# The first expert's first half on the first 384 tokens: one pass of 384 columns, or three of 128

## The chip, the cores and the metric

The kernel runs on one core of a Trainium2 chip. The metric is the device time of one execution in microseconds (us). Five engines work beside each other, each with a queue of its own that it takes in order: TensorE (PE, whose weight loads have a row of their own, PEld), VectorE (DVE), ScalarE (ACT), GpSimd (POOL) and SyncE (SP), which here issues all DMAs.

## The reference

Attention with a decay, a mixture of eight experts whose weights for each token are balanced over all tokens, and a gated layer behind it:

```python
scores = scale * q @ k.T + (cum[:, None] - cum[None, :]); causal mask
attn = softmax(scores);  x = attn @ v            # 2 batches, 8 heads, 576 tokens, head size 64
P = balance(exp(x @ w_gate))                     # 1152 tokens x 8 experts, 8 rounds over rows and columns
for e in range(8):
    out += P[:, e:e+1] * (relu(x @ w1[e]) @ w2[e])   # 512 -> 1024 -> 512
h = out @ w_in;  g = h * tanh(softplus(h));  return g @ w_out
```

All numbers are 32-bit. To keep precision at TensorE's faster number type, an operand is split into a high and a low part, and a product is three matmuls: high x high, low x high, high x low.

## The kernel before

Attention goes by query tiles: ten, five for each batch. Eight hold 128 rows, and one of each batch holds 64. Each tile has four units of two heads, so there are 40 units, and the loop in line 702 goes in half units: steps `s` = 0 to 87, `pi, a = divmod(s, 2)`. Tile `ti` has the steps 8 ti to 8 ti + 7. In the text the tiles are counted from one: the first has the steps 0 to 7. The program is written out in this order, and each engine takes its part of it in order. A step issues the exponential of the step before (ACT), the score matmuls (PE, then a masked reduction on DVE), dummy matmuls, one filler piece (`fill`, line 650), and, in odd steps, the attention product of three units back (`attend`) and the transposes of two units back. Then come the splits, transposes and copies of the next tile's queries and keys (`prep`), and DMA loads.

Dummy matmuls multiply the identity with itself. `warm` (line 391) issues one or two in each of the first 16 steps, and `warm_late` (line 396) one in steps 17, 19, 21, 25 and 27.

The filler is work of the expert stage that is put between attention's matmuls. Its weights are those of the first half of the first expert (512 of 1024 hidden units), loaded in four parts of 512 KB (`Weights.load`, line 52) into two staging buffers (tag `stg`, one of which first holds the raw second query and key tile, `early`), and split in eight pieces by `split_w` (line 322): the high part on ACT or DVE, whichever `pick` thinks is freer, and the low part on DVE. Tokens go in chunks of 384, three query tiles each in the first chunk. `filler(c)` (line 604) can start when the last tile of chunk c is attended. For each of four blocks of 128 hidden units it issues 12 matmuls of 384 columns, three to a piece, then evicts them: ReLU on ACT, low part on DVE. Then, for each of three token tiles, four pieces of three 512-wide matmuls, and an eviction into `acc`. That is 28 pieces, one a step: steps 31 to 58 for chunk 0, from step 63 on for chunk 1. Chunk 2 follows behind attention (line 825).

The weights for the filler are loaded when unit 7 starts (step 14) and split one piece at a time in every second step from 24 on; the third and fourth part are loaded as the buffers come free (`wsplit`, line 680).

Of the kernel before, what the change touches and what calls it, by code (L numbers as in the profile page):

```python
# [8 lines left out]
F32 = mybir.dt.float32  # L9
FR = mybir.dt.float32r  # L10
AF = mybir.ActivationFunctionType
ALU = mybir.AluOpType
# [26 lines left out]
def f(ap):  # L39
    return ap.bitcast(F32)  # L40
# [43 lines left out]
def attention_moe_kernel(  # L84
# [44 lines left out]
    with ExitStack() as actx:  # L129
# [165 lines left out]
        def spent(engine, ns):  # L295
            busy[engine] += ns
# [6 lines left out]
        def evac(o, i, cols, scale=None):  # L303
            if pick(act=90 + 0.83 * cols, dve=90 + 1.05 * cols) == "act":
                if scale:
                    nc.scalar.activation(out=o, in_=i, func=AF.Copy, scale=scale)
                else:
                    nc.scalar.copy(out=o, in_=i)
            elif scale:
                nc.vector.tensor_scalar(out=o, in0=i, scalar1=scale, scalar2=None, op0=ALU.mult)  # L310
            else:
                nc.vector.tensor_copy(out=o, in_=i)
# [80 lines left out]
            for _ in range(n):  # L393
                nc.tensor.matmul(out=wt[:, :128], lhsT=idn, rhs=idn, start=True, stop=True)  # L394

        def warm_late(n):

            late = ps_f.tile([128, 512], F32, tag="fb", name="late")
            for _ in range(n):
                nc.tensor.matmul(out=late[:, :128], lhsT=idn, rhs=idn, start=True, stop=True)  # L400

        def scores_two(u, a):
            b, h, nk = u["b"], u["h"], u["nk"]
            slot, k0 = u["slots"][h // 4], kbase[b]
# [153 lines left out]
        def attend(u):  # L558
            n, nk, h, b, pT = u["n"], u["nk"], u["h"], u["b"], u["pT"]
            if h == 0:  # L560
                u["tile"]["x"] = ps_x.tile([128, 4, 128], F32, tag="x", name="x")
            x = u["tile"]["x"]
            nblk = (nk + 127) // 128
            for j in range(nblk):
                w = 128 if j == 4 else min(128, nk - 128 * j)
                for a in range(2):
                    nc.tensor.matmul(  # L567
                        out=x[64 * a:64 * a + 64, h // 2, :n], lhsT=vts[b, j][:w, h + a, :],
                        rhs=pT[:w, 128 * j + 64 * a:128 * j + 64 * a + 64] if n == 64 else pT[:w, a, j * n:(j + 1) * n],
                        start=j == 0, stop=j == nblk - 1,  # L570
                    )
            if h == H - 2:
                c, t0 = divmod(b * S + u["s0"], CH)
                nc.scalar.copy(out=xh[c][:, :, t0:t0 + n], in_=x[:, :, :n])
                nc.vector.tensor_tensor(
                    out=xl[c][:, :, t0:t0 + n], in0=x[:, :, :n], in1=f(xh[c][:, :, t0:t0 + n]), op=ALU.subtract
                )
                spent("act", 90 + 3.4 * n)
                spent("dve", 90 + 4.2 * n)
# [16 lines left out]
        def gate_end(c, lg):  # L596
# [4 lines left out]
            nc.vector.tensor_copy(out=gl, in_=lt[:, :, E:])  # L601
            nc.vector.tensor_tensor(out=P[:, 3 * c:3 * c + 3], in0=lt[:, :, :E], in1=gl, op=ALU.add)

        def filler(c):

            w = wts.slots[0]
            if c == 0:
                hs = [
                    tuple(t[2][:, i].rearrange("p (j t) -> p j t", j=3) for t in (xh, xl)) for i in range(4)
                ]  # L610
            else:
                hs = []
                for i in range(4):
                    h0, c0 = 3 * (i % 2), 576 + 128 * (i // 2)
                    hs.append(tuple(t[:, h0:h0 + 3, c0:c0 + 128] for t in (kt, kbf)))
            for i in range(4):
                fs = slice(i * 128, (i + 1) * 128)
                ph = ps_f.tile([128, 512], F32, tag="fb", name="ph")[:, :CH]
                for kk in range(KD):
                    for n, (wn, x) in enumerate((("w1h", xh), ("w1h", xl), ("w1l", xh))):  # L620
                        nc.tensor.matmul(  # L621
                            out=ph, lhsT=w[wn][kk][:, fs], rhs=x[c][:, kk],
                            start=(kk == 0 and n == 0), stop=(kk == KD - 1 and n == 2),
                        )
                    if kk == KD - 1:
                        hh, hl = hs[i]
                        p3 = ph.rearrange("p (j t) -> p j t", j=3)
                        nc.scalar.activation(out=hh, in_=p3, func=AF.Relu)
                        nc.vector.scalar_tensor_tensor(
                            out=hl, in0=p3, scalar=0.0, in1=f(hh), op0=ALU.max, op1=ALU.subtract  # L630
                        )
                        spent("act", 400)
                        spent("dve", 500)
                    yield
            for j in range(3):
                pa = ps_f.tile([128, 512], F32, tag="fb", name="pa")
                for i in range(4):
                    hh, hl = hs[i]
                    for n, (a_, wn) in enumerate(((hh, "w2h"), (hh, "w2l"), (hl, "w2h"))):
                        nc.tensor.matmul(  # L640
                            out=pa, lhsT=a_[:, j], rhs=w[wn][i],
                            start=(i == 0 and n == 0), stop=(i == 3 and n == 2),
                        )
                    if i == 3:
                        evac(acc[c * 3 + j], pa, 512)
                    yield
# [32 lines left out]

        def wsplit(i):  # L680
            wts.split(0, i // 2, i % 2, how=split_w)
            if i % 2 and i < 5:
                wts.load(0, i // 2 + 2, stage)

        (qs0, qt0), (ks0, kt0) = make_preps(0)
        qs0(0)
# [15 lines left out]
        for s in range(2 * nu + 8):  # L702
# [11 lines left out]
                scores(units[pi], a)  # L714
            if s < 16:
                warm((2,2,2,2,2,2,2,2,1,1,1,1,1,1,1,1)[s])
            elif s in (17,19,21,25,27):
                warm_late(1)
            fill()
            fills += ready  # L720
            ready = []
            if a and 3 <= pi < nu + 3:
                w = units[pi - 3]
                attend(w)
                if w["h"] == H - 2 and w["ti"] in (2, 6, 9):
                    c = (2, 6, 9).index(w["ti"])
                    gates.append(c)
                    if c < 2:
                        ready.append(filler(c))
                elif gates:  # L730
                    logits.append(gate(gates.pop(0)))
            elif logits:
                gate_end(*logits.pop(0))
# [31 lines left out]
                    kt_(1)  # L765
            if late_rows and s >= 2:
                late_rows.pop(0)()
            if a:
                continue
            s = pi  # L770
            if s == 3:
                nc.gpsimd.tensor_copy(out=wgc[:, :, 0, :], in_=wg)
                nc.gpsimd.tensor_tensor(out=wgc[:, :, 1, :], in0=wg, in1=f(wgc[:, :, 0, :]), op=ALU.subtract)
            if s == 7:
                wts.load(0, 0, stage)
                wts.load(0, 1, stage)
            if s == 8:
                cum_k(1, 0, 256)
            if s == 22:
                cum_k(1, 256, 576)  # L780
            if s >= 12 and wtasks:
                wtasks.pop(0)()
        while gates:
            logits.append(gate(gates.pop(0)))
        fill(2)
# [1098 lines left out]
```

## Time and profile before

| | us |
|---|---|
| median of three runs | 1094.47 |
| the three runs | 1094.47, 1094.21, 1099.45 |
| profiled execution, span | 1097.7 |
| PE busy | 1090.1 |
| DVE busy | 839.7 |
| ACT busy | 541.6 |
| POOL busy | 75.3 |

The rows are of one profiled execution; its time is given by the span from its first to its last instruction, and no row gives what lies around it. The attention stage ends near 168 us of the span; the expert stage and the gated layer fill the rest. The ends of matmuls are modelled, so PE looks busy also where it waits a little; the starts of matmuls, one behind the other, tell more.

### The profile page before, as it was taken

How to read it: one execution, taken by the hardware profiler on the slowest of the kernel's cores; microseconds unless marked ns; L12 is line 12 of the kernel's file. 1: busy time of each engine (PE TensorE's matmuls, PEld its weight loads, DVE VectorE, ACT ScalarE, POOL GpSimd, SP SyncE). 2: the span in 40 equal slices, each digit the busy share in tenths (PEclk: the TensorE clock that was granted, in tenths of full speed). 3: DMA queues.
4: the chain of work that ended last, by engine and by line, in shares of the span. 5: the costliest groups of instructions: out<-in, count | busy, mean ns of one | idle time of the engine just before them, and what ended most of it. 6: DMA issues, size and time to landing. Idle time of an engine off the chain costs nothing.

```text
span 1097.7 us, 18374 instructions
## 1 busy us (share of the span) xinstructions
PE 1090.1 (99%) x6838; PEld 970.0 (88%) x6838; DVE 839.7 (76%) x1891; ACT 541.6 (49%) x1287; POOL 75.3 (7%) x124
## 2 busy tenths in 40 slices
PE   9999999999999999999999999999999999999998
PEld 8788778988989899898989989898898989899997
DVE  7755646878797887977888796888877559778994
ACT  7756642354435252443524335252443448877881
POOL 6534420000000000000000000000000000000000
PEclk9799999999999999999999999999999999999999
DMA  6534302022342424325243343424323341261502
GB/s 147 134 78 108 87 11 87 1 89 78 123 135 77 144 83 149 121 87 158 91 151 98 127 137 109 153 85 147 102 100 96 106 162 42 76 202 51 171 1 87
DMA packets 103805, 114.98 MB, mean 105 GB/s; under 512 B 35236, under 2 KB 63860, under 8 KB 103716
## 3 DMA queue, kind: packets, MB, share of 16 engines
q1 hardware_dynamic: 103716, 113.81, 33.6%
q8 instruction: 54, 0.88, 0.3%
q14 instruction: 35, 0.29, 0.1%
HBM read 82.24 MB, written 27.07 MB: 100 GB/s over the span
## 4 chain that ended last, share of the span: by engine, by line
PE 98%; DVE 1%; ACT 1%; issue 0%; POOL 0%; DVEq 0%; POOLq 0%
PE bank L855 33%; PE bank L1265 29%; PE bank L1737 9%; PE bank L1647 4%; PE ph L825 3%; PE x L567 3%; PE bank L1576 2%; PE spare L1647 2%; PE pa L855 2%; PE pa L640 2%; PE ph L621 1%; PE sp L467 1%; PE pt L360 1%; PE pt L531 1%; PE wt L394 1%; PE sp L468 1%
## 5 line engine op out<-in xcount | busy, mean ns | idle before, releaser
L855 PE MATMUL bank<-w2h,big 128*128 128x512 f32 x924 | 300.2, 394 | 0.0
L855 PEld LDWEIGHTS bank<-w2h,big 128*128 128x128 f32 x924 | 173.8, 188 | 38.7 <-DVE hid_b L833 0.2
L855 PE MATMUL bank<-w2l,big 128*128 128x512 f32 x528 | 207.5, 393 | 0.0
L1294 ACT COPY snap<-bank 128x288 f32<-128x288 f32 x168 | 66.6, 396 | 175.2 <-PE bank L1265 174.8
L855 PEld LDWEIGHTS bank<-w2l,big 128*128 128x128 f32 x528 | 99.3, 188 | 20.9
L832 ACT ACTIVATE big<-c 128x288 fp32r<-128x288 f32 x168 | 74.9, 446 | 83.7 <-DVE c L1299 79.7
L833 DVE SCALAR_TENSOR_TENSOR big<-c,big 128x288 fp32r<-128x288 f32 x140 | 64.0, 457 | 57.1 <-ACT big L832 54.5
L1030 DVE SCALAR_TENSOR_TENSOR acc<-bank,P,acc 128x512 f32<-128x512 f32 x132 | 92.3, 744 | 18.8 <-PE bank L855 18.8
L1265 PE MATMUL bank<-tt,ss 128*128 128x288 f32 x672 | 103.2, 295 | 0.0
L1265 PE MATMUL bank<-xh,ss 128*128 128x288 f32 x448 | 103.1, 295 | 0.0
L1265 PEld LDWEIGHTS bank<-tt,ss 128*128 128x128 f32 x672 | 93.9, 188 | 0.0
L1299 DVE TENSOR_TENSOR c<-bank,snap 128x288 f32<-128x288 f32 x168 | 75.8, 451 | 20.1 <-PE bank L1265 19.7
L1011 ACT CAST hb<-da 128x512 fp32r<-128x512 f32 x38 | 23.7, 624 | 107.4 <-DVE da L986 96.0
L1265 PEld LDWEIGHTS bank<-xh,ss 128*128 128x128 f32 x448 | 76.6, 188 | 0.0
L1265 PE MATMUL bank<-xl,ss 128*128 128x288 f32 x224 | 66.5, 297 | 0.0
L1265 PE MATMUL bank<-xh,w1l 128*128 128x288 f32 x224 | 66.2, 296 | 0.0
L1265 PE MATMUL bank<-xl,w1h 128*128 128x288 f32 x224 | 66.2, 295 | 0.0
L1265 PE MATMUL bank<-xh,w1h 128*128 128x288 f32 x224 | 66.1, 295 | 0.0
L75 DVE TENSOR_TENSOR w2l<-stg,w2h 128x512 fp32r<-128x512 f32 x60 | 41.2, 689 | 14.6 <-ACT w2h L74 14.1
L855 PE MATMUL bank<-w2h,hid_b 128*128 128x512 f32 x132 | 51.7, 391 | 0.0
L511 POOL TENSOR_SCALAR p<-p,rs 128x256 f32<-128x256 f32 (+5 forms) x72 | 42.0, 595 | 68.7 <-DVE rs L507 47.5
L1265 PE MATMUL bank<-tt,w1h 128*128 128x288 f32 x224 | 46.3, 295 | 0.0
(314 smaller groups left out, 2467.4 us busy)
## 6 DMA issues: line engine op xcount, KB each, us to landing
stg<-in_moe_w_dram SPq DMA_DIRECT2D x64, 512.0 KB
wb<-w_in_b SPq DMA_DIRECT2D x42, 256.0 KB
raw<-in_moe_w_in_dram SPq DMA_DIRECT2D x16, 512.0 KB
raw<-in_moe_w_out_dram SPq DMA_DIRECT2D x16, 512.0 KB
w_in_b<-hb SPq DMA_DIRECT2D x18, 256.0 KB
w_out_h<-hb SPq DMA_DIRECT2D x16, 256.0 KB
w_out_l<-da SPq DMA_DIRECT2D x16, 256.0 KB
w_in_f<-da SPq DMA_DIRECT2D x12, 256.0 KB
```

What stands on the lines that cost most here:

```text
L75: (lo_engine or nc.vector).tensor_tensor(out=lo, in0=raw, in1=f(hi), op=ALU.subtract)
L511: nc.gpsimd.tensor_scalar(out=p[:n, a, :nk], in0=p[:n, a, :nk], scalar1=r[:n, a:a + 1], scalar2=1.0, op0=ALU.mult, op1=ALU.mult,)
L567: nc.tensor.matmul(out=x[64 * a:64 * a + 64, h // 2, :n], lhsT=vts[b, j][:w, h + a, :], rhs=pT[:w, 128 * j + 64 * a:128 * j + 64 * a + 64] ...
L832: nc.scalar.activation(out=hh, in_=ph, func=AF.Relu)
L833: nc.vector.scalar_tensor_tensor(out=hl, in0=ph, scalar=0.0, in1=f(hh), op0=ALU.max, op1=ALU.subtract)
L855: nc.tensor.matmul(out=pa, lhsT=a_[:, ts_], rhs=w[wn][ft_], start=(first and n == 0), stop=(last and n == 2),)
L1030: nc.vector.scalar_tensor_tensor(out=acc[t], in0=pa, scalar=P[:, t, e:e + 1], in1=acc[t], op0=ALU.mult, op1=ALU.add)
L1265: nc.tensor.matmul(out=by_chunk(out_) if len(v_.shape) == 3 else out_, lhsT=u, rhs=v_, start=first and m == 0, stop=m == 5, skip_group_che ...
L1294: nc.scalar.copy(out=t, in_=bank["x", g])
L1299: nc.vector.tensor_tensor(out=t, in0=bank[of, g], in1=snap[with_, g], op=ALU.add)
L1647: nc.tensor.matmul(out=out_, lhsT=a_(kk, pa), rhs=b_(kk, pb), start=first and q == 0, stop=q == 5, skip_group_check=True,)
L1737: nc.tensor.matmul(out=bk[b][:, cs], lhsT=a_[:, ts_], rhs=w[wn][i][:, cs], start=i == 0 and q == 0, stop=i == 3 and q == 2,)
```

## The change

Chunk 0 of the filler is now done by `filler_tile(j)`, once for each of the first three query tiles, as soon as that tile is attended. Each has eight pieces: four with 12 matmuls of 128 columns, after the last of which all 512 columns are evicted at once, and four with three 512-wide matmuls. They stand in steps 15 to 22, 23 to 30 and 31 to 38. Steps 39 to 62 have no piece. The weights are loaded in steps 3, 5, 11 and 14 and split in steps 7, 9, 11, 13, 15, 16, 18 and 20. `warm_late` is gone. Chunk 1 is as before.

```diff
--- before.py
+++ after.py
@@ -392,12 +392,6 @@
 
             for _ in range(n):
                 nc.tensor.matmul(out=wt[:, :128], lhsT=idn, rhs=idn, start=True, stop=True)
-
-        def warm_late(n):
-
-            late = ps_f.tile([128, 512], F32, tag="fb", name="late")
-            for _ in range(n):
-                nc.tensor.matmul(out=late[:, :128], lhsT=idn, rhs=idn, start=True, stop=True)
 
         def scores_two(u, a):
             b, h, nk = u["b"], u["h"], u["nk"]
@@ -601,18 +595,46 @@
             nc.vector.tensor_copy(out=gl, in_=lt[:, :, E:])
             nc.vector.tensor_tensor(out=P[:, 3 * c:3 * c + 3], in0=lt[:, :, :E], in1=gl, op=ALU.add)
 
+        def filler_tile(j):
+
+            w = wts.slots[0]
+            ts_ = slice(128 * j, 128 * j + 128)
+            hh, hl = (t[2][:, :, ts_] for t in (xh, xl))
+            ph = ps_f.tile([128, 4, 128], F32, tag="fb", name="ph")
+            for i in range(4):
+                fs = slice(i * 128, (i + 1) * 128)
+                for kk in range(KD):
+                    for n, (wn, x) in enumerate((("w1h", xh), ("w1h", xl), ("w1l", xh))):
+                        nc.tensor.matmul(
+                            out=ph[:, i], lhsT=w[wn][kk][:, fs], rhs=x[0][:, kk, ts_],
+                            start=(kk == 0 and n == 0), stop=(kk == KD - 1 and n == 2),
+                        )
+                if i == 3:
+                    nc.scalar.activation(out=hh, in_=ph, func=AF.Relu)
+                    nc.vector.scalar_tensor_tensor(
+                        out=hl, in0=ph, scalar=0.0, in1=f(hh), op0=ALU.max, op1=ALU.subtract
+                    )
+                    spent("act", 510)
+                    spent("dve", 600)
+                yield
+            pa = ps_f.tile([128, 512], F32, tag="fb", name="pa")
+            for i in range(4):
+                for n, (a_, wn) in enumerate(((hh, "w2h"), (hh, "w2l"), (hl, "w2h"))):
+                    nc.tensor.matmul(
+                        out=pa, lhsT=a_[:, i], rhs=w[wn][i],
+                        start=(i == 0 and n == 0), stop=(i == 3 and n == 2),
+                    )
+                if i == 3:
+                    evac(acc[j], pa, 512)
+                yield
+
         def filler(c):
 
             w = wts.slots[0]
-            if c == 0:
-                hs = [
-                    tuple(t[2][:, i].rearrange("p (j t) -> p j t", j=3) for t in (xh, xl)) for i in range(4)
-                ]
-            else:
-                hs = []
-                for i in range(4):
-                    h0, c0 = 3 * (i % 2), 576 + 128 * (i // 2)
-                    hs.append(tuple(t[:, h0:h0 + 3, c0:c0 + 128] for t in (kt, kbf)))
+            hs = []
+            for i in range(4):
+                h0, c0 = 3 * (i % 2), 576 + 128 * (i // 2)
+                hs.append(tuple(t[:, h0:h0 + 3, c0:c0 + 128] for t in (kt, kbf)))
             for i in range(4):
                 fs = slice(i * 128, (i + 1) * 128)
                 ph = ps_f.tile([128, 512], F32, tag="fb", name="ph")[:, :CH]
@@ -679,8 +701,9 @@
 
         def wsplit(i):
             wts.split(0, i // 2, i % 2, how=split_w)
-            if i % 2 and i < 5:
-                wts.load(0, i // 2 + 2, stage)
+
+        wload = {3: 0, 5: 1, 11: 2, 14: 3}
+        wstep = (7, 9, 11, 13, 15, 16, 18, 20)
 
         (qs0, qt0), (ks0, kt0) = make_preps(0)
         qs0(0)
@@ -714,18 +737,18 @@
                 scores(units[pi], a)
             if s < 16:
                 warm((2,2,2,2,2,2,2,2,1,1,1,1,1,1,1,1)[s])
-            elif s in (17,19,21,25,27):
-                warm_late(1)
             fill()
             fills += ready
             ready = []
             if a and 3 <= pi < nu + 3:
                 w = units[pi - 3]
                 attend(w)
+                if w["h"] == H - 2 and w["ti"] < 3:
+                    ready.append(filler_tile(w["ti"]))
                 if w["h"] == H - 2 and w["ti"] in (2, 6, 9):
                     c = (2, 6, 9).index(w["ti"])
                     gates.append(c)
-                    if c < 2:
+                    if c == 1:
                         ready.append(filler(c))
                 elif gates:
                     logits.append(gate(gates.pop(0)))
@@ -765,21 +788,20 @@
                     kt_(1)
             if late_rows and s >= 2:
                 late_rows.pop(0)()
+            if s in wload:
+                wts.load(0, wload[s], stage)
+            if s in wstep:
+                wtasks.pop(0)()
             if a:
                 continue
             s = pi
             if s == 3:
                 nc.gpsimd.tensor_copy(out=wgc[:, :, 0, :], in_=wg)
                 nc.gpsimd.tensor_tensor(out=wgc[:, :, 1, :], in0=wg, in1=f(wgc[:, :, 0, :]), op=ALU.subtract)
-            if s == 7:
-                wts.load(0, 0, stage)
-                wts.load(0, 1, stage)
             if s == 8:
                 cum_k(1, 0, 256)
             if s == 22:
                 cum_k(1, 256, 576)
-            if s >= 12 and wtasks:
-                wtasks.pop(0)()
         while gates:
             logits.append(gate(gates.pop(0)))
         fill(2)
```

SP's queue around step 3, before: `kb<-kt` and `qb<-qa` are the copies of keys and queries into second buffers, `v` is the load of the second tile's values.

```order
L331 DMA qb_156<-qa_153 64x512
L331 DMA kb<-kt 64x4x128
L157 DMA v<-in_v_dram 128x8x64
L331 DMA qb_154<-qa_151 64x512
L293 DMA qb_154<-cd 2x4x128
L331 DMA kb<-kt 64x4x128
```

And after, where `stg` is the staging buffer of the weights:

```order
L331 DMA kb<-kt 64x4x128
L157 DMA v<-in_v_dram 128x8x64
L61 DMA stg<-in_moe_w_dram 128x2x512
L331 DMA qb_154<-qa_151 64x512
L293 DMA qb_154<-cd 2x4x128
L331 DMA kb<-kt 64x4x128
L61 DMA stg<-in_moe_w_dram 128x2x512
```

The first weight load now stands between the value load and the query copy, the second three places on.

ACT in steps 7 to 9, before: `p` are the exponentials, `pT` an eviction of transposes, `hl` a split of the next queries.

```order
L492 ACTIVATE p,sums_147<-p,nmax 128x128
L308 COPY pT<-pt 128x2x128
L492 ACTIVATE p,sums_147<-p,nmax 128x128
L492 ACTIVATE p,sums_144<-p,nmax 128x256
L308 COPY pT<-pt 128x2x128
L316 CAST hl<-raw 128x8x64
```

And after:

```order
L486 ACTIVATE p,sums_147<-p,nmax 128x128
L308 COPY pT<-pt 128x2x128
L324 CAST big<-stg 128x512
L486 ACTIVATE p,sums_147<-p,nmax 128x128
L316 CAST hl<-raw 128x8x64
L486 ACTIVATE p,sums_144<-p,nmax 128x256
```

The first weight conversion (`big<-stg`) stands ahead of the exponential of step 7, and a query split has come from DVE to ACT.

PE from step 18 to 19 (third tile), before: `sp` are scores, `x` the attention product, `pt` transposes.

```order
L467 MATMUL sp<-kt,qa_152 128x384
L468 MATMUL sp<-kb,qb_155 128x384
L360 MATMUL pt<-idr,hl 128x128 x4
L467 MATMUL sp<-kt,qa_152 128x384
L468 MATMUL sp<-kb,qb_155 128x384
L400 MATMUL late<-idn 128x128
L567 MATMUL x<-pT,v 64x128 x4
```

And after, from the fourth narrow piece's end:

```order
L608 MATMUL ph<-xl,big 128x128
L608 MATMUL ph<-xh,big 128x128
L360 MATMUL pt<-idr,hl 128x128 x4
L461 MATMUL sp<-kt,qa_152 128x384
L462 MATMUL sp<-kb,qb_155 128x384
L623 MATMUL pa<-big,xh 128x512 x2
L623 MATMUL pa<-big,xl 128x512
L561 MATMUL x<-pT,v 64x128 x4
```

The dummy is gone, and the second layer (`pa`) starts four transposes and two score matmuls behind the first layer's last matmul (`ph`).

## Rows read from the trace of the kernel before

**Rows 1.** The page, sections 1 and 2.
```profile
PE 1090.1 (99%) x6838; PEld 970.0 (88%) x6838; DVE 839.7 (76%) x1891; ACT 541.6 (49%) x1287; POOL 75.3 (7%) x124
...
PEclk9799999999999999999999999999999999999999
```

**Rows 2.** Busy time by stretch: us, each engine's busy us, clock, DMA share, GB/s.
```profile
18.30:27.37 9.07, 9.07 (x82) 7.70 (x81) 6.61 (x27) 7.94 (x24) 3.27 (x7) 1.00 0.82 189
27.37:38.24 10.87, 10.55 (x109) 8.55 (x107) 9.17 (x32) 8.83 (x25) 6.95 (x11) 1.00 0.83 196
38.24:43.60 5.36, 4.41 (x42) 3.30 (x39) 4.56 (x14) 4.31 (x12) 3.89 (x7) 1.00 0.39 83
43.60:57.50 13.90, 13.90 (x95) 10.46 (x93) 8.59 (x26) 7.64 (x20) 6.21 (x11) 0.51 0.38 89
90.78:102.77 11.99, 11.99 (x90) 9.33 (x88) 8.23 (x33) 7.13 (x22) 6.17 (x11) 1.00 0.55 124
```

**Rows 3.** Chain of waits, filler and later work: start us, us, what.
```profile
155.97 1.41 PE pa L640 x6
...
170.06 2.09 PE ph L825 x12
```

**Rows 4.** Timeline of PE, third tile: start us, us, engine, line, operation.
```profile
28.16 0.38 PE L400 MATMUL late<-idn 128*128 128x128 f32 x2
28.49 0.66 PE L567 MATMUL x<-pT,v 128*64 128x128 f32 x8
```

**Rows 5.** Timeline of PE: transposes, 128-wide and 64-wide score matmuls.
```profile
10.32 0.88 PE L360 MATMUL pt<-idr,hl 128*128 128x128 f32 x8
11.03 0.29 PE L467 MATMUL sp<-kt,qa 128*128 128x128 f32 x1
...
12.19 0.28 PE L468 MATMUL sp<-kb,qb 96*128 96x128 f32 x1
12.31 0.66 PE L394 MATMUL wt<-idn 128*128 128x128 f32 x4
...
78.82 0.28 PE L415 MATMUL sp<-kt,qa 128*128 128x64 f32 x1
78.93 0.28 PE L415 MATMUL sp<-kb,qb 96*128 96x64 f32 x1
```

**Rows 6.** Timeline of PE, second, fourth and ninth tile.
```profile
20.57 0.51 PE L360 MATMUL pt<-idr,hl 128*128 128x128 f32 x4
...
43.11 0.50 PE L467 MATMUL sp<-kt,qa 128*128 128x512 f32 x1 [0.92 <-DVE nmax L480]
...
46.90 0.79 PE L467 MATMUL sp<-kt,qa 128*128 128x512 f32 x1
...
52.78 0.79 PE L467 MATMUL sp<-kt,qa 128*128 128x512 f32 x1
...
120.30 0.50 PE L467 MATMUL sp<-kt,qa 128*128 128x512 f32 x1
...
124.45 0.50 PE L467 MATMUL sp<-kt,qa 128*128 128x512 f32 x1
```

**Rows 7.** Timeline of DVE, fourth tile.
```profile
40.53 1.66 DVE L328 TENSOR_TENSOR big<-stg,big 128x512 fp32r<-128x512 f32 x1
```

**Rows 8.** Source L328, low parts of the splits: ns min/median/max, first and last start.
```profile
L328 DVE TENSOR_TENSOR big<-stg,big x8: 676/693/1657, 40.5 to 77.7; 128x512 fp32r<-128x512 f32 x8
```

**Rows 9.** Timeline of SP's queue: issue of DMAs.
```profile
15.51 1.64 SPq L157 DMA_DIRECT2D v<-in_v_dram  x1
...
55.94 0.39 SPq L61 DMA_DIRECT2D stg<-in_moe_w_dram  x1
```

**Rows 10.** Timeline of ACT, first tile.
```profile
14.17 0.57 ACT L308 CAST kt<-pt 128x512 fp32r<-128x512 f32 x1
...
18.84 0.40 ACT L492 ACTIVATE p<-p,nmax 128x128 f32<-128x128 f32 x1
```

**Rows 11.** DMA from 55 to 61 us, 40 slices of 0.15 us.
```profile
GB/s 12 142 148 109 26 0 0 0 0 0 0 0 0 96 177 109 0 191 369 382 396 369 396 396 287 188 113 27 123 0 0 0 0 0 0 0 0 0 0 0
```

## The prediction

> **What bounds the kernel now.** I read the page first. PE is busy for 99% of the span and its granted clock is full in every slice but the second [rows 1]: a kernel bound by TensorE gains from work taken off PE, or from clock, and from little else. The change lies in the attention stage, so I cut that stage into stretches, one for each query tile (a tile is eight steps, s = 0 to 87) [rows 2]. In the fourth tile's stretch, 43.60 to 57.50, the clock is 0.51: the lower level, 1.2 GHz. In the seventh tile's stretch, 90.78 to 102.77, DVE works 8.23 us and ACT 7.13 us of 12.0, so neither is far behind PE. Third, the chain of waits gives the filler's price now: twelve 384-wide matmuls take 2.09 us, 0.174 each, and six 512-wide ones 1.41 us, 0.235 each [rows 3]. Then the timeline of PE for what is narrower, for the dummy matmuls and for the slow clock [rows 4 to 6], and last the queues that the moved weight work passes [rows 7 to 11].
>
> **The filler's first layer.** Before, chunk 0 takes 4 x 4 x 3 = 48 matmuls of 384 columns: 48 x 0.174 = 8.4 us. After, three tiles take 48 each of 128 columns: 144. Columns are the same, matmuls and weight loads three times as many. What does one cost? Two rows are near. A 128-wide score matmul starts at 12.19 and what follows it at 12.31: 0.12 [rows 5]. Four 64-wide ones, of the same number type, start 0.11 apart (78.82, 78.93), though they stream half the columns. So below some width the step no longer shrinks. Cheapest is the 128-wide transpose: eight from 10.32 to 11.03, 0.089 each. I take 0.111: 16.0 us, that is +7.6 (bounds: 0.089 gives 12.8, +4.4; 0.12 gives 17.3, +8.9). The Trainium skill ("TensorE: Matmul & The Clock Gate", section "Back-to-back issue gap") gives a sustained step of about 81 ns at 128 columns for pairs of load and matmul; as an estimate from it 144 would take 11.7 us, +3.3. This case's rows at 0.089 to 0.12 lie above it, and the sum keeps 0.111.
>
> **The second layer.** 36 matmuls of 512 columns before and after: nothing. But before, each quarter of the hidden layer was evicted four steps ahead of its use. Now the four are evicted together, 512 columns on ACT and then on DVE, and the first 512-wide matmul stands one step behind, after four transposes and two score matmuls. Such evictions take about 0.6 us each (an ACT conversion of 128x512 takes 0.57 [rows 10]), so the low part is ready some 1.4 us behind the last narrow matmul where both queues are free. PE gets to it after 0.36 (four transposes at 0.089 [rows 5]) + 0.45 (two score matmuls of 384 columns and 0.1 for the change of kind) + 0.47 (two 512-wide) = 1.28. With something queued ahead it waits. From 0 to 1.2 us a tile; I take 0.5, so +1.5 for three.
>
> **The dummy matmuls.** Five go. One starts at 28.16 and the first attend matmul behind it at 28.49 [rows 4]: 0.33. About 0.1 of that belongs to the change from one kind of matmul to the other and stays, so I take 0.24: 5 x 0.24 = -1.2 (bound -1.6).
>
> **The clock and the stall before it.** At 40.53 DVE has a weight split of 1.66 us [rows 7]; behind it the score reduction is late, and PE stands 0.92 us before 43.11 [rows 6]. Right after that the clock falls. After the change this place has filler pieces in every step and no split. The stall goes, -0.9. What the clock costs: a pair of heads at the lower level takes 52.78 - 46.90 = 5.9 us. The same work at full clock in the ninth tile takes 124.45 - 120.30 = 4.15, less two pieces of 0.52, 3.1. That is 2.8 of 5.9, and over the 13.9 us at the lower level [rows 2] 6.6 at most. Some of the work there, the chunk's gate and the loads of narrow weights, gains less, so I take -5.5 (bounds 0 and -6.6: nothing, if the clock falls there all the same).
>
> **The weights move forward.** The first load now stands in SP's queue right behind a V load [rows 9]: that is issued at 15.51 and holds the queue for 1.64 us, so ours goes at about 17.2, and ahead of a copy of queries. How long does such a load take? The one issued at 55.94 in an empty queue moves its bytes from about 57.5 to 59.0 [rows 9, 11]: 3.1 us. Behind the V bytes ours lands at 20.3 to 21.5, say 21.0. Its first split is in ACT's order right ahead of an exponential that started at 18.84 [rows 10]. ACT therefore stands about 2 us; DVE's half of the split follows, then DVE's reduction for step 8, and behind both the splits of the next queries and their transposes, which PE started at 20.57 [rows 6]: 21.0 + 0.6 (ACT) + 0.7 (DVE) + 0.5 (the reduction, half as many columns, an estimate) + 0.7 (a split of the queries, as long as a short one of the weights) = 23.5. PE is late by about 2.7 us (0 if the load lands by 18.8; 4 at the late end). Seven more splits fall into steps 9 to 20, DVE's part being 0.68 to 1.66 each [rows 8]. In the stretches 18.30 to 38.24 DVE already works 15.8 of 19.9 us [rows 2], but the pieces lengthen steps 15 to 20 by some 7 us (four of 1.33, two of 0.71), which covers most of them; what is left is in the bound of 4. The second load passes the copies and raw loads for the third tile, which are wanted eight steps later; the third and fourth wait in SP for a buffer that the splits free two steps before. POOL's queue gets nothing new. The choice between ACT and DVE for the high parts comes out six to two instead of four to four.
>
> The split at 40.53 takes 1.66 us, where the median of the eight is 0.69 [rows 7, 8]. The Trainium skill ("SBUF — State Buffer", on the port pair that VectorE and GpSimd share) says that a VectorE operation with two SBUF inputs and a GpSimd operation that reads SBUF exclude each other, and the second waits for the first to end. By that rule the change moves eight such splits into the stretches where POOL works most, and some would be longer by up to 1 us; the case's one long row agrees, and no run here shows the moved ones.
>
> **The cover that goes.** Steps 39 to 58 lose all their pieces, and steps 39 to 62 now have none. I have counted that as a saving at full price. It isn't in the seventh tile: 12.0 us less eight pieces of 0.71 leaves PE 6.3 us of work, while DVE has 8.23 [rows 2]. The second tile, with the same widths, dummies and no filler, took 9.1 us. So I take 8.6 instead of 6.3: +2.3 (0 to 3).
>
> **The sum.** +7.6 + 1.5 - 1.2 - 0.9 - 5.5 + 2.7 + 2.3 = +6.5 us. The profiled span is 1097.7, 3.2 us above the median of the runs (1094.47); the slowest run shown took 1099.45. What lies around the span is not in the rows, and I leave it out. If the excess of 3.2 us is time at the lower clock, the median has less of it to get back, and the result is 1097.7 + 6.5 = 1104.2; if it is of another kind, 1094.47 + 6.5 = 1101. I forecast 1102, with 1098 to 1106 for this case alone. A difference of 0.5%, 5.5 us, is what a measurement of this kernel can tell from no change.
>
> **Rivals.** *The clock falls in the emptied stretch.* From 78.82 to the filler of chunk 1 in step 63 PE would have only narrow scores, attends and transposes. For: the fall at 43.6 came in steps without filler, after a stall of under 1 us, and lasted 14 us until pieces came [rows 2, 6]; where PE waits for DVE, as in the seventh tile, there are many such stalls. Against: the clock stayed full from 18.30 to 38.24, with only dummies for filler [rows 2]. Price: from 78.82 to 102.77 are 24.0 us, less seven pieces of 0.52 and nine of 0.71 some 14 us of PE work; a pair goes from 3.1 to 5.9, 1.9 times, so at the lower level +12.6 at most, of which about half hides under DVE's 8.23. With +7 it is about 1109.
>
> *About nothing.* The narrow step is 0.089 (-3.2), and the load lands before its split (-2.7): 1102 - 5.9 = 1096. For it: transposes do go at 0.089. Against: the 64-wide row, and the V load ahead in the queue. The 81 ns of the Trainium skill, by themselves, would end at 1102 - 4.3 = 1098.
>
> *Faster.* PE's row hides room. Its ends are modelled, so that it never looks idle, but the weight loads are busy for only 8.55 of 10.87, 3.30 of 5.36 and 10.46 of 13.90 us in the three stretches from 27.37 to 57.50 [rows 2]: 7.8 us without a load. If PE there waits for ACT, DVE and POOL, the pieces fall into these holes and cost that much less, while steps 39 to 58 save their full price. Then it is 1102 - 7.8 = 1094, and with the narrow step and the load both at their good ends 1088, so 1086 to 1094. It is faster from about 13 us of such help in all. Against: the only stall of PE near 1 us that a row there names is the 0.92 [rows 6], and weight loads also stand still under wide matmuls.
>
> **Chances.** Forecast 0.36, the fall in the emptied stretch 0.26, about nothing 0.20, faster 0.18. Slower by over 0.5% (above 1099.9): 0.33 of the first and all but 0.01 of the second, 0.58. Faster (below 1089): half of the last and 0.04 of the third, 0.13. Within: the rest, 0.29. With every term at its good end the sum is -4.7, with every one at its bad end +17; the range 1090 to 1111 takes in most of both, and leaves out the best end of the faster case and a fall that lasts the whole emptied stretch.
>
> **What would show it.** Right: 144 narrow matmuls 0.11 apart; ACT standing about 2 us before its first weight conversion, near 19 us, with PE idle a little later; clock 1.00 from 24 to 60; the seventh tile's stretch at 8 to 9 us with DVE as the waiter; attention ending some 6 us later than now, and everything behind it unchanged. Wrong: narrow matmuls at 0.09 or less; no wait for the weights' DMA; pieces that fill holes, so that the steps 15 to 38 grow by much less than 24 us; or a clock below full anywhere else than at the start.

## The result and the profile after

The changed kernel takes 1111.32 us (median of four runs, 1110.23 to 1112.42), the kernel before on the same chip 1094.40. The ratio is 1.0149 (95% interval 1.0127 to 1.0171): 16.9 us slower. The forecast was 1102, so the sign was right and the size less than half of what came; 1111.3 lies just outside the range. The rival with a falling clock (1109) came nearer than the forecast, but as the experiments show it is only part of the answer.

The profiled execution took 1111.63 us, with a span of 1109.8: 1.8 us lie around the span. Its page says that PE is as busy as before, in 99% of the span, with 86 instructions more [rows 1]:

```profile
PE 1098.6 (99%) x6924; PEld 979.4 (88%) x6924; DVE 839.3 (76%) x1890; ACT 542.6 (49%) x1286; POOL 74.5 (7%) x124
```

The busy time by stretch, after (columns as in [rows 2]), cut at the places where PE waits or its clock changes:

```profile
20.57:23.52 2.95, 0.10 (x2) 0.03 (x1) 1.75 (x6) 2.24 (x7) 0.00 (x0) 1.00 0.93 250
23.52:31.00 7.48, 7.48 (x40) 6.24 (x41) 5.37 (x20) 5.83 (x16) 3.09 (x6) 0.54 0.59 128
31.00:34.94 3.94, 3.79 (x37) 3.39 (x36) 3.67 (x11) 2.21 (x6) 1.09 (x2) 1.00 0.84 242
34.94:52.88 17.94, 17.94 (x163) 15.32 (x161) 11.17 (x33) 11.90 (x30) 7.44 (x12) 1.00 0.33 82
52.88:74.65 21.77, 21.77 (x213) 17.52 (x209) 11.86 (x34) 10.48 (x26) 9.35 (x15) 1.00 0.20 43
...
96.25:104.75 8.50, 7.78 (x111) 6.79 (x110) 4.05 (x19) 5.40 (x16) 5.03 (x8) 1.00 0.45 100
104.75:109.20 4.45, 3.06 (x25) 2.10 (x23) 2.91 (x17) 3.34 (x13) 3.41 (x5) 1.00 0.76 180
109.20:116.10 6.90, 6.85 (x40) 5.96 (x41) 3.50 (x17) 5.00 (x15) 2.76 (x6) 0.51 0.63 148
```

Two stretches are at the lower clock of 1.2 GHz, 7.48 us behind the wait of the second tile and 6.90 us in the seventh, 14.4 us in all. The third and the fourth tile (34.94 to 52.88 and 52.88 to 74.65) are at full clock, so the fall that began at 43.6 in the profile before is not there; whether the change took it away is asked of the first experiment. The ends of the stretches give the whole account in time. Step 10's transposes start at 23.52 instead of 20.57; the last score pair of step 63, where nothing of the change is left, at 125.09 instead of 112.51, 12.6 us later; the span is longer by 12.1.

**The start.** The queue of SP, then ACT, DVE and PE of the same execution (start us, us, engine, line, operation; the wait before it in brackets). SP:

```profile
15.56 1.07 SPq L157 DMA_DIRECT2D v<-in_v_dram  x1
16.68 0.57 SPq L61 DMA_DIRECT2D stg<-in_moe_w_dram  x1
```

ACT:

```profile
21.08 0.62 ACT L324 CAST big<-stg 128x512 fp32r<-128x512 f32 x1 [2.14 <-DMA stg<-in_moe_w_dram]
```

DVE:

```profile
21.73 0.69 DVE L328 TENSOR_TENSOR big<-stg,big 128x512 fp32r<-128x512 f32 x1 [3.94 <-ACT big L324]
22.34 0.42 DVE L474 CUSTOM_DVE_ANT_0 p<-sp,mask 128x256 f32<-128x256 f32 x1
...
22.68 0.69 DVE L320 TENSOR_TENSOR hl<-raw,hl 128x512 fp32r<-128x512 f32 x1
23.29 0.15 DVE L497 TENSOR_SCALAR rs<-sums 128x6 f32<-128x6 f32 x1
```

PE:

```profile
23.52 0.51 PE L360 MATMUL pt<-idr,hl 128*128 128x128 f32 x4 [2.85 <-DVE rs L497]
```

Read down, it is the chain that the prediction wrote: the load goes behind the V load, ACT stands 2.14 us for it, DVE does the split, the reduction and the queries' split, and PE is 2.95 us late. The releaser named at 23.52 is L497, a small operation at 23.29, but by its operand (`hl`) what PE needs is the split that ends just before. What the prediction left out is the row 23.52:31.00 above. Its price can be read at the score matmul of step 14, which started at 25.28 before:

```profile
31.17 0.36 PE L461 MATMUL sp<-kt,qa 128*128 128x256 f32 x1
```

That is 5.9 us later. From step 10's transposes to this matmul it is 7.65 us (23.52 to 31.17), and it was 4.71 (20.57 to 25.28): 2.95 us of the delay is the wait, and 2.9 comes behind it, where PE has no idle time and the clock is low.

**The pieces.** The narrow matmuls of tile 1 (PE, same columns; each is paired with its weight load):

```profile
35.55 0.39 PE L608 MATMUL ph<-xh,big 128*128 128x128 f32 x2
35.78 0.28 PE L608 MATMUL ph<-xl,big 128*128 128x128 f32 x1
35.89 0.39 PE L608 MATMUL ph<-xh,big 128*128 128x128 f32 x2
```

Three start every 0.34 (35.55 to 35.89), 0.113 each; I took 0.111. And the second layer's first piece beside its next one:

```profile
42.04 0.73 PE L623 MATMUL pa<-big,xh 128*128 128x512 f32 x2
42.77 0.50 PE L623 MATMUL pa<-big,xl 128*128 128x512 f32 x1
...
45.00 0.63 PE L623 MATMUL pa<-big,xh 128*128 128x512 f32 x2
45.47 0.39 PE L623 MATMUL pa<-big,xl 128*128 128x512 f32 x1
```

The low part is wanted at the third matmul; it starts 0.73 behind the first in the one piece and 0.47 in the other, so the joint eviction seems to cost 0.26 here. The waits of the weight loads say the same for all tiles together, in their columns of us in total, times and longest: 1.3 us at most.

```profile
PEld pa L623 <- DVE xl L614: 1.0, 3, 0.4
...
PEld pa L623 <- ACT xh L613: 0.3, 1, 0.3
```

**The emptied stretch.** POOL and PE in the seventh tile:

```profile
106.40 1.26 POOL L320 TENSOR_TENSOR hl<-raw,hl 128x512 fp32r<-128x512 f32 x1
...
107.93 1.26 POOL L320 TENSOR_TENSOR hl<-raw,hl 128x512 fp32r<-128x512 f32 x1
```

```profile
106.31 0.28 PE L462 MATMUL sp<-kb,qb 96*128 96x256 f32 x1
107.72 0.53 PE L360 MATMUL pt<-idr,hl 128*128 128x128 f32 x4 [1.12 <-POOL hl L320]
...
109.25 0.68 PE L360 MATMUL pt<-idr,hl 128*128 128x128 f32 x4 [0.20 <-POOL hl L320]
```

The engine that I had expected PE to wait for there was DVE. It is POOL: its split of the next tile's queries takes 1.26 us, as it did before (1.27), but the pieces that stood over it are gone. The sixth tile gets 3.5 us shorter (96.25 to 104.75 against 78.82 to 90.78) where eight pieces or 4.4 us were taken, and the seventh, from which eight pieces or 5.7 us were taken, only 0.6 (11.40 against 11.99). The eighth, up to the last score pair of step 63, loses three pieces or 2.1 us and gets 0.8 shorter (8.94 against 9.74); there too PE waits for POOL:

```profile
119.44 0.54 PE L360 MATMUL pt<-idr,hl 128*128 128x128 f32 x4 [0.63 <-POOL hl L320]
```

So 0.9, 5.1 and 1.3 us of the pieces' price don't come back in the three tiles, 7.3 in all. Of the 5.1, the clock can be 3.4 at most, an estimate from 6.90 us at 0.51 of full speed.

### The profile page after: what moved, and what is told of

It reads as the page before. It is cut to its first block, busy times and chain, and to the rows that moved or that the text cites. A ratio compares the mean times of both kernels' runs of the same rounds, so it can differ in the third digit from the quotient of the medians.

```text
span 1109.8 us, 18546 instructions
## 1 busy us (share of the span) xinstructions
PE 1098.6 (99%) x6924; PEld 979.4 (88%) x6924; DVE 839.3 (76%) x1890; ACT 542.6 (49%) x1286; POOL 74.5 (7%) x124
## 4 chain that ended last, share of the span: by engine, by line
PE 97%; DVE 1%; ACT 1%; issue 1%; POOL 0%; DMA 0%; SPq 0%; DVEq 0%; ACTq 0%; POOLq 0%
PE bank L877 33%; PE bank L1287 28%; PE bank L1759 9%; PE bank L1669 4%; PE ph L847 3%; PE x L561 2%; PE bank L1598 2%; PE spare L1669 2%; PE pa L877 2%; PE ph L608 1%; PE sp L461 1%; PE pt L360 1%; PE pt L525 1%; PE wt L394 1%; PE sp L462 1%; PE pa L623 1%
## 5 line engine op out<-in xcount | busy, mean ns | idle before, releaser
L308 ACT COPY pT<-pt 128x512 f32<-128x512 f32 (+4 forms) x51 | 24.4, 505 | 45.2 <-PE pt L525 33.5
```

## Experiments

**The kernel before, once more.** No edit.

> The kernel before, unchanged, to see which of its executions have the slow clock from 43.6 to 57.5 us. Theory A (the fall of the clock there is a thing of the one profiled execution, and the median executions lack it, so that there was nothing to win): most executions near 1094.4 us, the profile of one of them with clock above 0.9 in all of the stretch from 40 to 60 us and a span near 1092.5. Theory B (the fall is in every execution, and the excess of the profiled span is something else): the profile shows the half-clock stretch of 10 to 14 us also where the time is 1094.

1094.44 us, ratio 1.0002 (0.9985 to 1.0019). With all runs of this kernel in the three sets of experiments there are 64 executions, each with its mean granted clock (one, at 2319.44 us, is left out below):

| mean clock | executions | us |
|---|---|---|
| 0.999 to 1.000 | 45 | 1094.0 to 1095.3 |
| 0.998 | 8 | 1094.8 to 1095.9 |
| 0.995 | 1 | 1097.8 |
| 0.994 | 9 | 1099.3 to 1099.5 |

The execution profiled this time is of the second kind (columns as in [rows 2]):

```profile
40.00:43.60 3.60, 2.64 (x31) 1.85 (x28) 3.53 (x10) 2.56 (x7) 2.17 (x3) 1.00 0.31 71
43.60:47.20 3.60, 3.60 (x33) 2.87 (x31) 2.54 (x8) 1.99 (x6) 2.58 (x4) 0.53 0.48 99
47.20:52.00 4.80, 4.80 (x47) 3.64 (x47) 4.01 (x11) 4.42 (x12) 2.70 (x6) 1.00 0.60 163
```

The clock comes back at 47.2, before the first filler piece (51.73); in [rows 2] it stays low to 57.5. The profile that the prediction read was of the fourth kind: its span of 1097.7 and the 1.8 us around it make 1099.5, the slowest of the three runs shown, and its mean clock is 0.994. By time and mean clock 9 executions of 63 are like it, and they are 5.0 us longer (1099.4 less 1094.4), which is near the 5.5 that I took. The median execution has a mean clock of 0.999 or more, so it has no such stretch, and nothing to win back there.

**Narrow matmuls alone.** The kernel before, chunk 0's first layer in three parts of 128 columns at its old place:

```diff
-                for kk in range(KD):
-                    for n, (wn, x) in enumerate((("w1h", xh), ("w1h", xl), ("w1l", xh))):
+                three = (("w1h", xh), ("w1h", xl), ("w1l", xh))
+                parts = 3 if c == 0 else 1
+                cw = CH // parts
...
-                            out=ph, lhsT=w[wn][kk][:, fs], rhs=x[c][:, kk],
+                            out=ph[:, js], lhsT=w[wn][kk][:, fs], rhs=x[c][:, kk, js],
```

> The kernel before, in which chunk 0's first layer is done in 144 matmuls of 128 columns (nine to a piece) at its old place, instead of 48 of 384. Theory A (0.111 us each, and PE is the bound there): +7.6 us, 1102. Theory B (the narrow ones go into room that PE has): +3 us or less, 1097. At 0.089 each it would be +4.4.

1101.47 us, ratio 1.0060 (1.0040 to 1.0080): +7.2, with the clock at 0.999 to 1.000 in all five executions. The largest term of the sum stands, as the first theory had it. The run says nothing on the room under PE's row that the faster rival spoke of, for the narrow matmuls stand here behind that place. One wait and one stretch more are of use:

```profile
43.07 0.50 PE L467 MATMUL sp<-kt,qa 128*128 128x512 f32 x1 [0.92 <-DVE nmax L480]
```

```profile
38.22:55.02 16.80, 15.39 (x166) 11.26 (x162) 14.24 (x38) 12.01 (x31) 10.83 (x19) 1.00 0.48 117
```

The wait of 0.92 us is there as in [rows 6], and the clock behind it is full. The three profiles with the old order of splits shown so far all have the wait; 13.9 us at the lower clock, 3.6 and none stand behind it.

**The weights early, alone.** The kernel before with the new steps of loads and splits, and nothing else:

```diff
+        wload = {3: 0, 5: 1, 11: 2, 14: 3}
+        wstep = (7, 9, 11, 13, 15, 16, 18, 20)
...
-            if s >= 12 and wtasks:
-                wtasks.pop(0)()
```

> The kernel before with the weights' loads and splits moved as in the change, and its own filler and dummies kept. Theory A (wait for the load 3 us, slow clock behind it 3 us, later steps a little freer of splits): 1094.4 + 5.5 = 1100. Theory B (the moved weight work costs nothing of its own, all of it lies beside PE): 1094.5. Theory C (eight splits in steps 7 to 20 also hold up DVE and ACT for long): 1104 or more.

1101.97 us, ratio 1.0066 (1.0041 to 1.0090): +7.7. PE's two long waits:

```profile
24.83 0.72 PE L360 MATMUL pt<-idr,hl 128*128 128x128 f32 x4 [4.16 <-DVE rs L503]
```

```profile
38.76 0.69 PE L467 MATMUL sp<-kt,qa 128*128 128x384 f32 x1 [2.14 <-DVE nmax L480]
```

Behind each the clock is low for a while (24.00 to 31.00 at 0.54, 37.00 to 45.00 at 0.57). The expectation's nearest theory had 1100 and one wait. The second wait, at 38.76, is not in the changed kernel, where pieces stand beside the later splits; that they cover it there is likely and not shown. So this run shows that early weights are dear, but it is not the price that they have in the changed kernel.

**The first load earlier still.** The changed kernel, first load in step 0:

```diff
-        wload = {3: 0, 5: 1, 11: 2, 14: 3}
+        wload = {0: 0, 5: 1, 11: 2, 14: 3}
```

> The changed kernel with its first weight load issued in step 0 in place of step 3. Theory A (the wait for that load costs twice: PE stands 2.95 us, and then runs 7 us at the lower clock, which costs another 3): both go, about 6 us below the changed kernel, 1105 us. Theory B (only the wait itself counts, the clock falls there anyway): 1108. Theory C (the load now delays the first tiles' copies and raw loads as much): 1111, with PE standing for a copy or for the queries of the third tile instead.

1110.29 us, ratio 1.0141 (1.0115 to 1.0166): no difference from the changed kernel that can be told (four runs from 1109.14 to 1112.58, against 1110.23 to 1112.42). As the third theory had it, the wait has a new name. PE:

```profile
18.30 0.36 PE L461 MATMUL sp<-kt,qa 128*128 128x256 f32 x1
21.90 0.55 PE L462 MATMUL sp<-kb,qb 96*128 96x256 f32 x1 [3.23 <-DMA kb<-kt]
```

The copy of the keys now stands behind the weights' load in the queue, and ACT still waits for the weights (1.50 us). Issued in step 3 the weights are late; issued in step 0, ahead of the copies, the copies are late, and the weights still are.

**The first splits later.** The changed kernel with its loads, but the first four splits in steps 10, 11, 13 and 14:

```diff
-        wstep = (7, 9, 11, 13, 15, 16, 18, 20)
+        wstep = (10, 11, 13, 14, 15, 16, 18, 20)
```

> The changed kernel with its loads where they are and the first four splits in steps 10, 11, 13 and 14 instead of 7, 9, 11 and 13, so that the load has landed when ACT comes to them. Theory A (the wait of 2.95 us and the slow clock of 7 us behind it, which costs 3 more, hang together): both go, 1111.3 - 6 = 1105, clock full from 20 to 90 us. Theory B (the clock falls in the second tile anyway, for the load's bytes hold up copies or the splits hold up DVE): 1108 or above.

1108.49 us, ratio 1.0123 (1.0105 to 1.0141), 2.8 us less than the changed kernel. By stretch:

```profile
18.30:23.50 5.20, 5.20 (x46) 4.41 (x45) 3.86 (x13) 4.56 (x15) 1.41 (x3) 1.00 1.04 293
23.50:31.00 7.50, 6.62 (x52) 5.32 (x52) 5.74 (x21) 5.19 (x15) 3.49 (x6) 1.00 1.21 229
...
104.00:111.00 7.00, 6.90 (x43) 5.74 (x42) 4.54 (x20) 4.68 (x14) 2.95 (x6) 0.51 0.72 166
```

The one long wait is gone and so is the lower clock up to 31; the second fall is untouched. The score matmul of step 14 shows what that brings in this execution:

```profile
26.12 0.35 PE L461 MATMUL sp<-kt,qa 128*128 128x256 f32 x1
```

It is 5.05 us earlier than in the changed kernel, and the last score pair of step 63 is still 4.6 us earlier (120.53). So both the wait and the slow clock behind it go, as the first theory had it, and most of the hoped 6 us came. The median has only 2.8 of it, the second theory's number: this execution is the fastest of four, at 1107.21; another is at 1107.40, and two, with a mean clock of 0.995, are at 1109.59 and 1110.44. What those two lost was not profiled.

**The pieces spread.** The changed kernel with the pieces of the second and third tile begun after steps 38 and 46, so that the stretch has work again:

```diff
+            if s in (38, 46):
+                ready.append(filler_tile((38, 46).index(s) + 1))
...
-                if w["h"] == H - 2 and w["ti"] < 3:
-                    ready.append(filler_tile(w["ti"]))
+                if w["h"] == H - 2 and w["ti"] == 0:
+                    ready.append(filler_tile(0))
```

> The changed kernel with the same pieces, but those of the second and third query tile in steps 39 to 46 and 47 to 54 instead of 23 to 30 and 31 to 38. Theory A (the emptied steps cost about 4 us of lost cover and 3 us of slow clock from 109 to 116): 1111.3 - 6 = 1105, with no half-clock stretch beyond 100 us. Theory B (PE is the bound wherever the pieces stand, so moving them does nothing): 1111. Theory C (without pieces the fourth tile now loses its clock, as the kernel before does in some executions): about 1110, with the half-clock stretch near 50 us.

1107.37 us, ratio 1.0110 (1.0094 to 1.0126): 3.9 us less than the changed kernel.

```profile
23.50:31.00 7.50, 6.55 (x35) 5.47 (x36) 5.97 (x23) 6.00 (x19) 3.09 (x6) 0.56 0.55 120
...
96.00:104.00 8.00, 8.00 (x72) 7.60 (x72) 2.95 (x15) 3.41 (x11) 2.69 (x5) 1.00 0.58 135
104.00:111.00 7.00, 6.96 (x50) 5.23 (x50) 4.24 (x15) 4.22 (x12) 2.66 (x5) 1.00 0.40 94
```

The mirror image of the run before: the second fall is gone, the first stays.

**Both.** The two edits together:

```diff
+        wstep = (10, 11, 13, 14, 15, 16, 18, 20)
...
+            if s in (38, 46):
+                ready.append(filler_tile((38, 46).index(s) + 1))
```

> Both of the two before at once: pieces spread and the first splits later. If the two causes are independent, the savings add: 1111.3 - 12 = 1099.5, which is the kernel before + 7 for the narrow matmuls + 0.7 for the late eviction - 1.2 for the dummies, less than 1 us apart. If they share one cause, it is no better than the better of the two.

1103.74 us, ratio 1.0081 (1.0064 to 1.0097), 7.6 less than the changed kernel where the two alone gave 2.8 and 3.9, and the clock at 0.998 to 1.000. The savings add, more or less, which speaks for two separate causes; but 1103.74 is 4.2 above the 1099.5 that was expected, since each saving was hoped at 6. What is left over the narrow kernel of the second experiment is 2.3 us. Half of it is in the second tile: the same score matmul of step 14, in that kernel and in this one.

```profile
25.28 0.35 PE L467 MATMUL sp<-kt,qa 128*128 128x256 f32 x1
```

```profile
26.55 0.35 PE L461 MATMUL sp<-kt,qa 128*128 128x256 f32 x1
```

1.3 us by there (0.8 in the profile of the run with later splits alone), and 2.5 by the last score pair of step 63 (114.47 and 116.93). So the early weights still cost about 1 us in the second tile. The rest was not parted by a run; cover is in it, for the eighth tile has three pieces or 2.1 us less than in the narrow kernel and is only 0.8 shorter, with PE waiting for POOL in it:

```profile
111.09 0.54 PE L360 MATMUL pt<-idr,hl 128*128 128x128 f32 x4 [0.55 <-POOL hl L320]
```

**The two small gains, at the old place.** The kernel before without its dummies; with its splits in odd steps, where no reduction of a head pair stands behind them; and with both. The two edits:

```diff
-            elif s in (17,19,21,25,27):
-                warm_late(1)
...
+            if a and pi >= 12 and wtasks:
+                wtasks.pop(0)()
...
-            if s >= 12 and wtasks:
-                wtasks.pop(0)()
```

> The kernel before without its five dummy matmuls (steps 17, 19, 21, 25 and 27), nothing else changed. My theory takes each at 0.24 us of PE's time: 1.2 us less, so about 1093.3 against 1094.5, and the wait of about 0.9 us before the score matmul of step 24 stays in the profile. Rival: the dummies stood in gaps that PE has anyway, so nothing is saved (1094.3 to 1094.7) and what the run with both edits gained (1.1 to 1.4 us) came from the splits alone. A second rival: without them the clock falls in the third tile, and the time is 1096 or more.

1094.81 us, ratio 1.0003 (0.9991 to 1.0016): no difference that can be told, as the first rival had it. But the second rival is not out: only four of the 12 executions have a mean clock of 0.999 or more, against 17 of the 23 of the kernel before that ran beside them. These four are at 1093.95 to 1094.16, those 17 at 1094.03 to 1094.77, so at full clock the dummies may cost 0.3 us, far from the 1.2 forecast. PE in the third tile without the dummy of step 17 (the rows with it are [rows 4]):

```profile
28.16 0.34 PE L468 MATMUL sp<-kb,qb 96*128 96x384 f32 x1
28.66 0.66 PE L567 MATMUL x<-pT,v 128*64 128x128 f32 x8 [0.17 <-DVE pT L312]
```

From the score to the attend matmul it is 0.50 us, where with the dummy it was 0.51 (27.98 to 28.49 in the profile of before): this one dummy stood over a wait for DVE.

> The kernel before with its eight weight splits one half-step later, in the odd steps, where no head pair's score reduction waits behind them; the five dummies stay. By my prediction's term the wait of 0.92 us before the score matmul of step 24 goes: about 1093.6, and no execution shows the 14 us at the lower clock that followed that wait in the profiled one. Rival: what the split delayed is delayed elsewhere, and the time stays at 1094.3 to 1094.7, so that the gain of the run with both edits came from the dummies.

1094.04 us, ratio 0.9995 (0.9985 to 1.0005), no difference that can be told. The wait of 0.92 us before the score matmul at 43.11 (step 27 by the rows; the two expectations say 24) is gone from its profile, and 0.49 us for POOL stands a little later. The long fall is absent from all 11 executions (clock 0.998 and more), but with 9 in 63 before, 11 without one prove little.

> The kernel before with its weight splits in odd steps from 25 on (away from the query splits on POOL) and without the five late dummies: an attempt at a better kernel. Theory A (the stall of 0.92 us goes and each dummy is 0.24 us of PE): 1094.4 - 2.1 = 1092.3. Theory B (without the dummies the clock falls in the third or fourth tile in most executions): 1098 to 1100, clock 0.994.

1093.29 us (12 runs), ratio 0.9984 (0.9973 to 0.9995), 1.3 us less than before (1094.6 without the one at 2319.44): the one kernel here that is faster than both, by little.

```profile
41.82 0.50 PE L467 MATMUL sp<-kt,qa 128*128 128x512 f32 x1
...
44.60 0.50 PE L360 MATMUL pt<-idr,hl 64*128 64x64 f32 x4 [0.72 <-POOL hl L320]
```

The wait of 0.92 before the score matmul is gone (that matmul starts at 41.82 instead of 43.11), and 0.72 of POOL stands a little later. Only the interval of both edits together lies clear of 1. What each brings by itself is within the noise of its own run, so these runs don't show whether the two help each other.

## Why the prediction fell short

| term | forecast, us | found, us | from |
|---|---|---|---|
| narrow matmuls | +7.6 | +7.2 | measured alone |
| joint eviction | +1.5 | at most 1.3 | weight loads' waits after |
| dummies gone | -1.2 | +0.3 (-1.0 to +1.8) | measured alone, old place |
| stall at 43.11 gone | -0.9 | -0.5 (-1.6 to +0.5) | measured alone, old place |
| clock at 43.6 to 57.5 | -5.5 | 0 in the median execution | 63 executions of before |
| weights at the start | +2.7 | +5.9 at step 14 | rows after |
| cover gone | +2.3 | +7.3 in three tiles | rows after |

**The step that failed is the clock**, in three terms. The first is the gain. "I take -5.5" for the stretch 43.60 to 57.50 was about right for the profiled execution and wrong for the kernel: the median execution has no such stretch. The prediction had seen that the span lay 3.2 us above the median, said that in one case "the median has less of it to get back", and then took a value between the two cases. It left out what lies around the span; with about 1.8 us there (1.6 to 2.0 in the runs here), the profiled execution was the slowest run shown, and the case of 1104.2 would have come to 1106.0. The sum without the term is +12.0, 1106.5. The Trainium skill ("TensorE: Matmul & The Clock Gate", Part 1) says that the number of matmuls which a kernel runs at the lower clock at its start changes from run to run. The 63 executions show as much for a fall in the middle of a kernel, with mean clocks from 0.994 to 1.000 of one program.

The second is the start, and the third the emptied stretch: in both the prediction's sum priced waits (+2.7, +2.3) and put the lower clock behind them at nothing.

**The start.** The mechanism came as written, load, ACT, DVE and PE, to within 0.3 us (2.95 against 2.7). But I priced the wait alone. The clock is 0.54 for 7.48 us behind it, and the forecast "clock 1.00 from 24 to 60" is wrong for its first 7 us. By step 14 the wait has cost 2.95 us and what comes behind it 2.9 more. In all four executions of the changed kernel the mean clock is 0.993 or 0.994. Later splits took both away in the profiled execution (5.05 us by step 14), and gave 2.8 in the median.

**The emptied stretch.** The rival was right that the clock falls there, and wrong on its size: 6.9 us low, not 24. The forecast's 2.3 us stood for the seventh tile alone, with PE waiting for DVE; by the rows it is 5.1 there, POOL is what PE waits for, and the sixth and eighth tile add 2.2. Spread pieces gave 3.9 us back.

**The third and fourth tile.** They took 39.7 us (17.94 and 21.77) where they took 27.7 in kernels at full clock (10.87 in [rows 2], 16.80 in the narrow kernel): 12.0 more. The price of their sixteen pieces, at 1.36 and 0.71, less the one of 1.0 that stood there in the narrow kernel, is 15.5. So 3.5 us came back, with what the joint evictions cost taken off, a little more than the 2.1 that the prediction took for dummies and stall, and far from the 7.8 of the faster rival. At the old place neither edit alone gave a saving that can be told.

**What held.** The narrow step (0.113 against 0.111), the queue and its landing time (ACT's first conversion starts at 21.08, the load was expected at 21.0), and all but 0.5 us of what comes behind step 63 (12.6 us late there, 12.1 at the end). The warning that splits moved forward would grow by VectorE's and GpSimd's common port came true for one of eight; the longest of L328 after, and the split on POOL beside it:

```profile
37.42 1.36 DVE L328 TENSOR_TENSOR big<-stg,big 128x512 fp32r<-128x512 f32 x1 [1.16 <-ACT big L324]
```

```profile
36.95 1.28 POOL L320 TENSOR_TENSOR hl<-raw,hl 128x512 fp32r<-128x512 f32 x1 [2.08 <-ACT hl L316]
```

By the Trainium skill ("SBUF — State Buffer", section "Who interferes with whom") a VectorE instruction with two SBUF inputs contends with a GpSimd instruction that reads SBUF, and the later one waits. That would have this operation wait for POOL's to end at 38.23 and then take its usual 0.69, to 38.92; the row ends at 38.78, so it agrees to 0.14.

**Open.** Of the 16.9 us, 7.2 and 7.6 are shown by experiment and 2.1 is what is left. With the 7.2 of the narrow matmuls the rows make it 7.2 + 5.9 + 7.3 - 3.5 = 16.9, but the last three are readings of one execution of each kernel, and that they meet the median to a tenth is luck. In the seventh tile the wait and the clock behind it were not parted, and why the same wait is followed by the lower clock in one execution and not in another stays open.

## What to carry to other kernels

Before a gain is read from one profiled execution, compare its own time with the median of the runs: a stretch at the lower clock may belong to that execution and not to the kernel. Price a wait of PE with what the clock does behind it, and price filler that is moved by the waits that it stood over, engine by engine, POOL's too. What an edit saves at its old place need not be what it saves in the changed kernel: there, pieces may stand over the same waits.

## What was not expected of the hardware

The same program has, by time and mean clock, some 14 us at the lower clock in 9 of 63 executions, less in 9, and none in 45; 5.0 us lie between the first kind and the last. The two of them that were profiled, with 13.9 and 3.6 us, have the same wait of 0.92 us ahead of it. In the changed kernel the waits of 2.85 and 1.12 us come with 14.4 us at the lower clock, and its four executions lie within 2.2 us. A matmul of 128 columns with its weight load starts 0.113 behind the last, one of 64 columns 0.11 [rows 5], and a row of transposes 0.089.
